# Second-layer experts ranked on chip and run as a straight list of token tiles

## The chip, the cores and the metric

One core of one Trainium2 chip runs the whole program. The core has five engines with queues of their own: TensorE (PE, matmuls and transposes), VectorE (DVE), ScalarE (ACT), GpSimd (POOL) and SyncE (SP, which here only issues transfers). The metric is the device time of one execution in microseconds; the time of a kernel is the median over its runs.

## What is computed

Three stages follow each other: block-causal attention, a first layer that takes the maximum of three products, and a second layer in which each token goes to one of eight experts, or to none.

```python
# attention: B=4, H=8, S=576, D=64, blocks of 64
scores = where(block_i >= block_j, q @ k.T / sqrt(D), -1e9)
x = softmax(scores) @ v                       # -> 2304 tokens x 512
# first layer (d_ff 768)
h = maximum(maximum(x @ w1, x @ w2), x @ w3)
x = h @ w_out
# second layer: N=2304, D=512, E=8, F=1024
do_compute = (x @ w_skip) > 0                 # other tokens pass through
logits = xc @ w_gate
e_idx = argmax(logits, axis=1)
gate_w = softmax(logits)[e_idx]
for e in range(E):                            # tokens of this expert
    y[mask] = gate_w * (maximum(xc[mask] @ w1[e], 0) @ w2[e])
out[do_compute] = xc + y
```

How many tokens an expert gets depends on the inputs. With the inputs of these runs, worked out from the reference, 532 of 2304 tokens are computed, and the experts hold 0, 0, 153, 69, 60, 116, 17 and 117 of them.

## The kernel before

Products keep more of fp32's precision by splitting each operand into a rounded part `hi` and a rest `lo`, and adding three products (hi x hi, hi x lo, lo x hi). A tile is 128 tokens.

The first layer runs in nine chunks of 256 tokens (0 to 8), and its steps are interleaved with the attention of the following chunks by a scheduler that fills all engines. `moe_steps` lists the steps of a chunk: `m_h` (L339, 18 steps of 12 matmuls), `m_logits` (L363), `m_y` (L375, two `y` tiles written to the DRAM tensors `x2` and `out`), `r_gate` (L393, chooses expert and gate) and `r_rank` (L423). `r_rank` gives each token a place in its expert's part of a DRAM table (2304 places for each expert) and scatters token number and gate there; `cum16` holds the counts so far. Chunk 7's two `y` are put off into chunk 8, behind its `m_h`, where they cover chunk 8's ranking (L466 to L475).

The second layer is the class `Moe2`. A weight quarter is 512 x 512 numbers, 1 MB; an expert has four (s = 0, 1 of w1 and 2, 3 of w2). SP loads a quarter into `raw` (L606), ACT makes `hi` (L651), and DVE and POOL each make half of `lo` (L655). While chunk 8's `m_h` runs, `before_step` (L623) loads the first quarters, in the order of expert numbers, and splits the first six: those of expert 0 and half of expert 1. The rings hold six `hi`, six `lo` and six `raw`.

After the last `y`, the counts come out of a matmul (L565), every engine loads all eight into registers (L753), POOL gathers the tokens of the first experts from `x2` (L663), and then a loop that is written out over the eight experts runs under branches: an expert with no token is skipped, one with more than 128 gets a second tile (L783), one with more than 256 a loop. The work on a tile is `products` (L690): the token tile is transposed on PE (L671), ACT and DVE make its two parts out of PSUM (L673, L674), 24 matmuls make the hidden tile in two halves, each half is put through a relu (L703, L710) and transposed and split in the same way, and 24 matmuls make `psy`. The expert's own quarters 2 and 3 are split at the head of its tile and quarters 0 and 1 of the next expert inside it. `finish` (L726) adds and scatters the result to `out` by POOL.

From `_run` on (L737) the order is the one in which the code is written; each engine takes its instructions in that order.

Of the kernel before, what the change touches and what calls it, by code (L numbers as in the profile page):

```python
# [21 lines left out]
P = 128  # L22
# [26 lines left out]
def kernel(  # L49
# [23 lines left out]
    table = dram.tile([NE * CAP, 2], F32, name="table")  # L73

# [10 lines left out]
    counts = const.tile([1, NE], I32, name="counts")  # L85
# [5 lines left out]
def _moe1_phase(tc, nc, const, small, g):  # L91
# [3 lines left out]
    wr_sb, x2, table, out, counts = (g[n] for n in ("wr_sb", "x2", "table", "out", "counts"))  # L95
# [6 lines left out]
    with ExitStack() as st_y:  # L102
# [21 lines left out]
        hid = [[ypool.tile([P, NF, CH], F32R, tag=n, name=n) for n in ("h_h", "h_l")]]  # L124
# [238 lines left out]
        def m_logits(c, rd):  # L363
            h_h, h_l = hid[c // (NCH - 1)]
# [10 lines left out]
        def m_y(c, t, mid=None):  # L375
# [3 lines left out]
            h_h, h_l = hid[c // (NCH - 1)]  # L379
# [64 lines left out]
        def moe_steps(c):  # L444
# [11 lines left out]
            if c < NCH - 2:  # L456
                m_y(c, 0)
                yield
                r_gate(c, rd)
                m_y(c, 1)  # L460
                yield
                r_rank(c, rd)
            elif c == NCH - 2:
                r_gate(c, rd)
                yield
                r_rank(c, rd)  # L466
            else:
                r_gate(c, rd)
                m_y(c - 1, 0, lambda: r_rank(c, rd))
                yield  # L470
                m_y(c - 1, 1)
                yield
                m_y(c, 0)
                yield
                m_y(c, 1)  # L475
# [10 lines left out]
        def constants():  # L486
# [7 lines left out]
            nc.vector.tensor_copy(cum16, base8)  # L494
            nc.vector.tensor_copy(tri, g["cst_sb"][:, P:2 * P])
# [3 lines left out]

        queue = []  # L500
# [351 lines left out]
```

## Time and profile before

| | us |
|---|---|
| median of 3 runs | 754.44 |
| lowest and highest run | 746.52 and 754.82 |
| the profiled execution | 756.49 |
| its span, first to last instruction | 754.7 |
| PE busy in it | 683.6 (91%) |
| DVE, ACT, POOL busy | 474.8, 359.6, 332.6 |

In the profile, times count from the first instruction. "PEclk" is the clock that was granted to TensorE, as a share of full speed. "Idle before" names the time an engine stood still ahead of a row and what released it. An engine counts as busy while it executes an instruction, also when that instruction is held up by another engine.

### The profile page before, as it was taken

How to read it: one execution, taken by the hardware profiler on the slowest of the kernel's cores; microseconds unless marked ns; L12 is line 12 of the kernel's file. 1: busy time of each engine (PE TensorE's matmuls, PEld its weight loads, DVE VectorE, ACT ScalarE, POOL GpSimd, SP SyncE). 2: the span in 40 equal slices, each digit the busy share in tenths (PEclk: the TensorE clock that was granted, in tenths of full speed). 3: DMA queues.
4: the chain of work that ended last, by engine and by line, in shares of the span. 5: the costliest groups of instructions: out<-in, count | busy, mean ns of one | idle time of the engine just before them, and what ended most of it. 6: DMA issues, size and time to landing. Idle time of an engine off the chain costs nothing. (4 is left out here: it accounts for less than half of the span.)

```text
span 754.7 us, 13850 instructions
## 1 busy us (share of the span) xinstructions
PE 683.6 (91%) x4774; PEld 574.4 (76%) x4774; DVE 474.8 (63%) x1307; ACT 359.6 (48%) x941; POOL 332.6 (44%) x422
## 2 busy tenths in 40 slices
PE   7698978999999999999999999999999945988885
PEld 4456756688889889889979979989988834766663
DVE  5899995643456667576657658766547305466574
ACT  4565664243446455555445455644446114364451
POOL 4677775354445222312102133211109528487773
PEclk9989887599999999999999999999999986998899
DMA  7753441242132133322022153111027939757720
GB/s 193 200 159 127 128 132 41 69 123 77 50 99 57 35 102 80 117 99 64 26 64 66 33 147 120 39 64 48 18 95 263 341 113 311 265 173 262 261 80 30
DMA packets 82435, 89.98 MB, mean 119 GB/s; under 512 B 10588, under 2 KB 59132, under 8 KB 82344
## 3 DMA queue, kind: packets, MB, share of 16 engines
q1 hardware_dynamic: 78680, 83.39, 35.5%
q0 software_dynamic: 2624, 5.45, 2.2%
q8 instruction: 47, 0.77, 0.4%
q14 instruction: 44, 0.36, 0.1%
q10 hardware_dynamic: 1040, 0.01, 0.1%
HBM read 78.14 MB, written 11.96 MB: 119 GB/s over the span
## 5 line engine op out<-in xcount | busy, mean ns | idle before, releaser
L348 PE MATMUL ps_h<-x,w 128*128 128x256 f32 x1944 | 282.0, 295 | 1.9 <-DVE hm L355 1.7
L348 PEld LDWEIGHTS ps_h<-x,w 128*128 128x128 f32 x1944 | 254.1, 196 | 11.6 <-issue 5.3
L283 ACT ACTIVATE p<-sc,nm 64x288 f32<-64x288 f32 (+9 forms) x192 | 95.5, 500 | 54.0 <-DVE nm L280 12.4
L276 DVE TENSOR_REDUCE nm<-sc 64x1 f32<-64x288 f32 (+9 forms) x192 | 85.1, 450 | 50.0 <-PE sc L271 30.2
L316 PE MATMUL tp<-cst_sb,p 128*128 128x128 f32 (+1 forms) x480 | 91.4, 282 | 14.8 <-DVE r L299 4.9
L655 POOL TENSOR_TENSOR lo<-raw,hi 128x1024 fp32r<-128x1024 f32 x30 | 81.7, 2741 | 17.5 <-ACT hi L651 8.5
L316 PEld LDWEIGHTS tp<-cst_sb,p 128*128 128x128 f32 (+1 forms) x480 | 57.7, 145 | 36.2 <-issue 15.4
L333 PE MATMUL pv<-pT,vt 128*64 128x128 f32 (+1 forms) x960 | 77.2, 281 | 4.5 <-ACT pT L318 3.9
L360 POOL TENSOR_TENSOR h_l<-hm,h_h 128x256 fp32r<-128x256 f32 x54 | 43.6, 808 | 80.3 <-ACT h_h L359 74.0
L655 DVE TENSOR_TENSOR lo<-raw,hi 128x1024 fp32r<-128x1024 f32 x30 | 66.3, 2222 | 14.1 <-ACT hi L651 13.0
L302 POOL TENSOR_TENSOR p<-p,r 128x128 f32<-128x128 f32 (+8 forms) x72 | 58.9, 820 | 35.4 <-DVE r L299 26.4
L651 ACT CAST hi<-raw 128x2048 fp32r<-128x2048 f32 x30 | 56.4, 1903 | 31.0 <-PEq L783 17.8
L333 PEld LDWEIGHTS pv<-pT,vt 128*64 128x64 f32 x960 | 53.0, 142 | 22.5 <-issue 6.1
L244 POOL TENSOR_TENSOR kl<-kq,kh 64x512 fp32r<-64x512 f32 (+3 forms) x36 | 36.7, 1019 | 64.5 <-ACT kh L243 58.5
L318 ACT COPY pT<-tp 128x256 f32<-128x256 f32 (+4 forms) x112 | 44.7, 401 | 28.8 <-PE tp L316 27.9
L287 POOL MEMSET p<- 128x64 f32 (+1 forms) x96 | 14.3, 153 | 99.8 <-PE tp L316 91.5
L320 DVE COPY pT<-tp 128x256 f32<-128x256 f32 (+4 forms) x80 | 35.4, 447 | 29.0 <-PE tp L316 28.2
L265 PE MATMUL sc<-kn,kq 73*64 73x288 f32 (+4 forms) x96 | 46.5, 594 | 5.5 <-DMA kq<-in_kq_dram 5.2
L269 PE MATMUL sc<-kh,q 128*128 128x288 f32 (+9 forms) x144 | 48.5, 343 | 1.7 <-ACT p L283 1.7
L336 DVE TENSOR_TENSOR x<-pv,x 128x128 fp32r<-128x128 f32 (+1 forms) x80 | 21.6, 270 | 38.4 <-ACT x L335 38.4
L385 PE MATMUL ps_y<-wo_h,h_h 128*128 128x512 f32 x108 | 44.5, 412 | 0.0
L271 PE MATMUL sc<-kl,q 128*128 128x288 f32 (+9 forms) x144 | 43.5, 308 | 0.0
(146 smaller groups left out, 1149.1 us busy)
## 6 DMA issues: line engine op xcount, KB each, us to landing
raw<-in_m_w_dram SPq DMA_DIRECT2D x32, 1024.0 KB
raw<-in_w_dram SPq DMA_DIRECT2D x18, 512.0 KB
kq<-in_kqT_dram SPq DMA_DIRECT2D x16, 512.0 KB
vt<-in_v_dram SPq DMA_DIRECT2D x16, 320.0 KB
x<-y SPq DMA_DIRECT2D x18, 256.0 KB
out_dram<-y SPq DMA_DIRECT2D x18, 256.0 KB
raw<-in_w_out_dram SPq DMA_DIRECT2D x6, 512.0 KB
kq<-in_kqT_dram SPq DMA_DIRECT2D x8, 384.0 KB
```

What stands on the lines that cost most here:

```text
L265: nc.tensor.matmul(ps[:nq, 0:hi - lo], gd["raw"][0:KN, j, q0:q0 + nq], kn_all[hp][0:KN, j, lo:hi], start=True, stop=True)
L269: nc.tensor.matmul(ps[:nq, 0:hi - lo], gd["q1"][:, j, q0:q0 + nq], gd["kh"][:, j, lo:hi], start=True, stop=False)
L276: nc.vector.tensor_reduce(nm[:nq, n:n + 1], pss[n][:nq, 0:hi - lo], axis=AX.X, op=ALU.max, negate=True)
L283: nc.scalar.activation(pt[:nq, lo:hi], pss[n][:nq, 0:hi - lo], AF.Exp, bias=nm[:nq, 0:1], scale=0.125 if b == 0 else 1.0, accum_out=su[:nq ...
L302: nc.gpsimd.tensor_tensor(pt, pt, r[:nq, 0:1].to_broadcast([nq, nk]), op=ALU.mult)
L316: nc.tensor.transpose(tp[:, t, 0:nq], h["p"][:nq, (t0 + t) * P:(t0 + t + 1) * P], ident[:nq, :nq])
L318: nc.scalar.copy(pT[:, t0:t0 + n, 0:nq], tp[:, 0:n, 0:nq])
L333: nc.tensor.matmul(pv[64 * jj:64 * jj + 64, 0:nq], vt[:, t, 64 * jj:64 * jj + 64], hd[k - 1 + jj]["pT"][:, t, 0:nq], start=(t == 0), stop= ...
L348: nc.tensor.matmul(ps, a[:, d, :], x[:, d, :], start=(n == 0), stop=(n == 3 * ND - 1))
L385: nc.tensor.matmul(ps, a[:, f, hs], x[:, f, :], start=(n == 0), stop=(n == 3 * NF - 1))
L651: self.nc.scalar.copy(self.w(e, s)[0], self.raw_of(4 * e + s))
L655: eng.tensor_tensor(lo[:, r], self.raw_of(4 * e + s)[:, r], hi[:, r], op=ALU.subtract)
```

## The change

The second layer no longer runs over experts but over a list of token tiles. It is planned on DVE, from counts that a matmul with a full `ones` puts on all partitions:

- After chunk 6's ranking (1792 tokens) `Plan.rank` orders the experts by their count so far. The numbers of the first three go to SP's registers, and the weights of tiles 0 to 2 are loaded from addresses in these registers, while chunk 8 runs.
- After chunk 7's ranking `Plan.first` notes whether the first expert has at least 128 tokens by then. The rows of its first tile are read from the table and gathered from the first 2048 rows of `x2` during chunk 8 (`Moe2.first`). If it has fewer, that tile's result is sent out of range and its tokens are done again later.
- After chunk 8 `Plan.rest` makes the list of all remaining tiles: expert, place in the table, and the number of tiles.
- Seven tiles (`NS`) run in straight code: the early one, one each for the second and third expert, and four of the list. Any further tile runs in a loop, under the only branch left. Tiles of one expert no longer share its loaded weights.
- Quarters are taken in the order of `seq`, in which quarter 3 of a tile stands behind quarter 0 of the next. `split_hi` is written five and `split_lo` four quarters ahead; DVE now makes 320 of 512 columns of `lo` and POOL 192 (256 each for the first six).
- Chunk 7's `y` go back into chunk 7, and the second copy of the hidden tile (`hid`) goes.

```diff
-            if c < NCH - 2:
+            if c < NCH - 1:
                 m_y(c, 0)
                 yield
                 r_gate(c, rd)
                 m_y(c, 1)
                 yield
                 r_rank(c, rd)
-            elif c == NCH - 2:
...
+                if c >= NCH - 3:
+                    ps = ps_m.tile([P, NE], F32, tag="mo", name="ps_c")
+                    nc.tensor.matmul(ps, ones, cum16, start=True, stop=True)
+                    (plan.rank if c == NCH - 3 else plan.first)(ps)
             else:
                 r_gate(c, rd)
...
+                m_y(c, 0, lambda: r_rank(c, rd))
...
+        m2.first()
         for n in range(3 * NF):
             m2.before_step(n)
             run_moe()
         m2.before_step(3 * NF)
         with tc.manual_schedule():
+            run_moe()
+            run_moe()
+            m2.ready()
+            m2.run(run_moe)
...
+    def first(self, ps):
+        v = self.nc.vector
+        cnt = self.counts(ps, "key")
+        fl, c0 = self.tile("fl", [P, 2]), self.tile("c0", [P, NE])
+        v.tensor_tensor(c0, self.pm[:, 0, :], cnt, op=ALU.mult)
+        v.tensor_reduce(fl[:, 0:1], c0, axis=AX.X, op=ALU.add)
+        v.tensor_scalar(fl[:, 0:1], fl[:, 0:1], float(P), None, op0=ALU.is_ge)
+        v.tensor_scalar(fl[:, 1:2], fl[:, 0:1], -BIG, BIG, op0=ALU.mult, op1=ALU.add)
...
+    def rest(self, ps, pool):
...
+        v.tensor_tensor(big[0], st, inner(off), op=ALU.is_ge)
+        v.tensor_tensor(big[1], st, inner(end), op=ALU.is_ge)
+        v.tensor_tensor(big[0], big[0], big[1], op=ALU.subtract)
...
+        self.seq = [(0, 0), (0, 1), (0, 2)]
+        for k in range(1, self.NS):
+            self.seq += [(k, 0), (k - 1, 3), (k, 1), (k, 2)]
+        self.seq.append((self.NS - 1, 3))
...
+    def reg(self, ap, top):
+        return self.nc.values_load(ap, engines=[mybir.EngineType.SP], min_val=0, max_val=top)
...
+    def load_q(self, e, s, raw):
+        if s < 2:
+            src = self.m2_w1[bass.ds(e, 1), :, s * 512:(s + 1) * 512]
...
+    def first(self):
+
+        nc, plan = self.nc, self.plan
+        self.load_raws(3)
+        self.rows(0, self.reg(plan.pi[0:1, 3:4], (NE - 1) * CAP))
...
+        self.gather(0, NT - CH)
...
+    def split_lo(self, q, m):
+        (hi, lo), raw = self.w(q), self.raw_of(q)
+        for eng, a, b in ((self.nc.vector, 0, m), (self.nc.gpsimd, m, 512)):
+            eng.tensor_tensor(lo[:, :, a:b], raw[:, :, a:b], hi[:, :, a:b], op=ALU.subtract)
...
+    def ready(self):
+
+        ps = self.ps_m.tile([P, NE], F32, tag="mo", name="ps_c")
+        self.nc.tensor.matmul(ps, self.ones, self.cum16, start=True, stop=True)
+        self.g0()
+        self.plan.rest(ps, self.right)
+        for t in (1, 2):
+            self.rows(t, self.reg(self.plan.pi[0:1, 3 + t:4 + t], (NE - 1) * CAP))
+
+    def run(self, last_y):
...
+        self.index(1, 3)
+        self.gather(1)
+        self.gather(2)
...
+        for j, (k, s) in enumerate(self.seq):
+            if s == 0 and k > 0:
+                turn_h(k - 1, 1)
+            if s == 1 and k > 0:
+                turn_h(k, 0)
+            if s == 2 and 0 < k < NS - 1:
+                turn_x(k + 1)
...
+            mm(0, 6)
+            if (k, s) == (0, 1):
+                turn_h(0, 0)
+            if (k, s) == (0, 2):
+                turn_x(1)
...
+            mm(6, 12)
+            if 6 <= j + 5 < len(self.seq):
+                self.split_hi(j + 5)
+            if 6 <= j + 4 < len(self.seq):
+                self.split_lo(j + 4, 320)
...
+            if j < NS - 3:
+                t = 3 + j
+                self.expert[t] = self.reg(li[0:1, 2 * j:2 * j + 1], NE - 1)
+                self.rows(t, self.reg(li[0:1, 2 * j + 1:2 * j + 2], (NE - 1) * CAP + NT - P))
+            self.load_raws(j + 11)
...
+            if 6 <= j < 3 + NS:
+                self.gather(j - 3)
+        self.loop(T, h)
```

The change moves instructions. On PE, just behind the last `y` matmul of chunk 8, the kernel before has (the first operand behind an arrow is the moving one, the second the stationary one; `Two_h`, `Two_l` are the two parts of a transposed tile):

```order
L385 MATMUL ps_y<-wo_l,h_h 128x512
L565 LDWEIGHTS ones
L565 MATMUL ps_c<-cum_69,ones 1x8
L753 TENSOR_LOAD counts x8
L758 COMPARE_AND_BRANCH
L671 MATMUL psa_7844<-cst_sb,xgs_8294 128x128 x4
L758 UNCONDITIONAL_BRANCH x2
L763 COMPARE_AND_BRANCH
L687 MATMUL psa_7844<-hi_7835,Two_h 128x512 x4
```

and the changed kernel has there (`x0h`, `x0l` are the parts of the early tile `xg`, `h` a half of its hidden tile):

```order
L387 MATMUL ps_y<-wo_l,h_h 128x512
L824 LDWEIGHTS ones
L824 MATMUL ps_c<-cum_70,ones 128x8
L783 MATMUL pst_7870<-cst_sb,xg_7864 128x128 x4
L795 MATMUL psa_7868<-hi_7856,x0h 128x512 x4
L795 MATMUL psa_7868<-hi_7856,x0l 128x512 x4
L795 MATMUL psa_7868<-lo_8135,x0h 128x512 x4
L795 MATMUL psa_7869<-hi_7857,x0h 128x512 x4
L795 MATMUL psa_7869<-hi_7857,x0l 128x512 x2
L783 MATMUL pst_7870<-cst_sb,h_8590 128x128 x4
```

The register loads and branches are gone from there, the early tile's transposes follow the last `y` at once, and the first transposes of `h` stand a quarter and a half behind them.

On DVE, the kernel before has between chunk 8's last count and its first relu:

```order
L438 TENSOR_TENSOR cum_69<-cum_69,oh_8312 128x8 x2
L751 TENSOR_SCALAR tg<-tt 128x16
L752 CAST ti<-tt 128x16
L566 SCALAR_TENSOR_TENSOR counts<-cst_sb,ps_c 1x8
L753 TENSOR_LOAD counts x8
L757 MEMSET psy 128x512
L758 COMPARE_AND_BRANCH
L674 TENSOR_TENSOR Two_l<-psa_7844,Two_h 128x512
```

The changed kernel has in the same place the 26 operations of the list, of which the last rows are shown, then the two of `index`, and only then the relu that PE's transposes of `h` wait for:

```order
L654 TENSOR_REDUCE lf<-plan_8535 128x28
L655 TENSOR_TENSOR plan_8536<-plan_8534,d 128x224
L656 TENSOR_REDUCE lf<-plan_8536 128x28
L657 SCALAR_TENSOR_TENSOR lf<-steps,lf 128x28
L658 CAST li<-lf 128x56
L659 CAST li<-end 128x1
L660 TENSOR_SCALAR miss<-steps,end 128x28
L818 CAST ti<-tt 128x2
L819 TENSOR_SCALAR tg<-tt 128x2
L875 TENSOR_SCALAR h_8590<-psa_7868 128x512
L787 TENSOR_TENSOR Two_l<-pst_7870,Two_h 128x512
```

The list thus stands ahead of the index of the next gathers and of the first relu on the same queue.

On POOL, while chunk 8's first layer runs, the kernel before has splits of the first quarters and the `h_l` of chunk 8 alone:

```order
L439 DMA table<-pair,sloti 18432x2 x2
L655 TENSOR_TENSOR lo_8010<-raw_7832,hi_7835 128x1024
L360 TENSOR_TENSOR h_l<-hm_8006,h_h 128x256
L655 TENSOR_TENSOR lo_8045<-raw_7833,hi_7836 128x1024
L360 TENSOR_TENSOR h_l<-hm_8059,h_h 128x256
L655 TENSOR_TENSOR lo_8082<-raw_7834,hi_7837 128x1024
```

and the changed kernel has the gather of the early tile (`xg`) between them:

```order
L441 DMA table<-pair,sloti 18432x2 x2
L774 TENSOR_TENSOR lo_8135<-raw_7853,hi_7856 128x4x256
L774 TENSOR_TENSOR lo_8170<-raw_7854,hi_7857 128x4x256
L362 TENSOR_TENSOR h_l<-hm_8131,h_h 128x256
L774 TENSOR_TENSOR lo_8207<-raw_7855,hi_7858 128x4x256
L362 TENSOR_TENSOR h_l<-hm_8184,h_h 128x256
L777 DMA xg_7864<-x_63,tg 128x512
L362 TENSOR_TENSOR h_l<-hm_8240,h_h 128x256
```

The gather stands behind the third `lo`, and four of chunk 8's six `h_l` are behind it.

## Rows read from the trace of the kernel before

**Rows 1.** Busy us (x instructions) by stretch: PE, PEld, DVE, ACT, POOL, PEclk, DMA share, GB/s.

```profile
150.00:556.00 406.00, 402.87 (x3298) 356.15 (x3298) 250.50 (x901) 200.52 (x642) 116.53 (x230) 1.00 0.24 72
556.00:593.00 37.00, 34.90 (x289) 32.83 (x287) 20.11 (x40) 17.30 (x24) 26.03 (x14) 0.95 0.76 258
613.00:632.00 19.00, 1.44 (x5) 1.10 (x6) 5.03 (x6) 5.22 (x5) 12.42 (x10) 0.57 0.56 173
```

**Rows 2.** Timeline, last y to first tile: start us, us, engine, line, [idle before, releaser].

```profile
612.23 0.39 PE L385 MATMUL ps_y<-wo_l,h_h 128*128 128x512 f32 x1
...
612.70 0.59 ACT L388 COPY y<-ps_y 128x512 f32<-128x512 f32 x1 [3.53 <-PE ps_y L385]
612.75 0.15 DVE L566 SCALAR_TENSOR_TENSOR counts<-cst_sb,ps_c 1x8 int32<-1x8 f32 x1 [4.03 <-PE ps_c L565]
...
617.05 0.48 DVE L757 MEMSET psy<- 128x512 f32 x1 [4.16 <-issue]
617.59 1.00 POOL L663 DMA_INDIRECT xgs<-x,tg  x1 [16.30 <-DVEq L758]
...
621.77 0.75 DVE L728 SCALAR_TENSOR_TENSOR xo<-psy,tt,xgs 128x512 f32<-128x512 f32 x1 [4.23 <-DMA xgs<-x,tg]
...
631.65 2.05 PE L687 MATMUL psa<-hi,Two_h 128*128 128x512 f32 x4 [4.42 <-PEq L783]
```

**Rows 3.** Timeline, the last matmuls.

```profile
747.61 1.09 PE L687 MATMUL psy<-lo,Two_h 128*128 128x512 f32 x4
```

**Rows 4.** Timeline of PE inside expert 2's second tile.

```profile
652.05 1.09 PE L687 MATMUL psb<-hi,Two_h 128*128 128x512 f32 x4
...
652.98 0.63 PE L687 MATMUL psb<-hi,Two_l 128*128 128x512 f32 x2
...
654.34 1.09 PE L687 MATMUL psb<-lo,Two_h 128*128 128x512 f32 x4
```

**Rows 5.** The tile raw, who reads it: ns min/median/max, first and last start.

```profile
L651 ACT CAST hi<-raw x30: 1889/1902/1934, 562.7 to 734.6; 128x2048 fp32r<-128x2048 f32 x30
L655 DVE TENSOR_TENSOR lo<-raw,hi x30: 1215/1254/6023, 569.5 to 736.6; 128x1024 fp32r<-128x1024 f32 x30
L655 POOL TENSOR_TENSOR lo<-raw,hi x30: 2361/2422/3442, 569.7 to 739.2; 128x1024 fp32r<-128x1024 f32 x30
```

**Rows 6.** Timeline, DVE and POOL at the same time.

```profile
665.20 0.69 DVE L703 TENSOR_SCALAR h<-psa 128x512 f32<-128x512 f32 x1 [0.31 <-PE psa L687]
...
697.28 1.23 DVE L655 TENSOR_TENSOR lo<-raw,hi 128x1024 fp32r<-128x1024 f32 x1 [0.32 <-ACT hi L651]
697.47 1.86 POOL L663 DMA_INDIRECT xg<-x,tg  x1 [0.30 <-issue]
...
736.63 6.02 DVE L655 TENSOR_TENSOR lo<-raw,hi 128x1024 fp32r<-128x1024 f32 x1
736.84 4.73 POOL L655 TENSOR_TENSOR lo<-raw,hi 128x1024 fp32r<-128x1024 f32 x2
```

**Rows 7.** Timeline of POOL, first and last of 11 indirect DMAs, first `lo`.

```profile
662.55 0.99 POOL L729 DMA_INDIRECT out_dram<-xo,ti  x1 [8.99 <-DVEq L787]
663.72 6.77 POOL L655 TENSOR_TENSOR lo<-raw,hi 128x1024 fp32r<-128x1024 f32 x2 [0.18 <-ACT hi L651]
...
735.65 1.19 POOL L729 DMA_INDIRECT out_dram<-xo,ti  x1 [0.31 <-issue]
```

**Rows 8.** Timeline of DVE, two dependent small operations.

```profile
597.58 0.17 DVE L418 TENSOR_SCALAR se<-se 128x2 f32<-128x2 f32 x1
597.78 0.17 DVE L419 RECIPROCAL pair<-se 128x2 f32<-128x2 f32 x1
```

**Rows 9.** Timeline, chunk 8's last table scatter and the index made from the table.

```profile
600.32 0.98 POOL L439 DMA_INDIRECT table<-pair,sloti  x1 [0.30 <-issue]
...
608.47 0.17 DVE L751 TENSOR_SCALAR tg<-tt 128x16 int32<-128x16 f32 x1 [9.46 <-DMA tt<-table]
```

**Rows 10.** DMA queues from 556 to 640: GB/s in 40 equal slices.

```profile
GB/s 26 375 101 21 407 395 388 283 49 402 92 407 72 281 277 349 376 386 395 387 385 231 179 1 198 163 145 119 131 8 131 205 203 198 135 365 385 384 388 371
```

More of the change, by code (lines that the diff above doesn't have):

```diff
@@ L94, in _moe1_phase @@
     tri, ones, tid, cum16, wp = (g[n] for n in ("tri", "ones", "tid", "cum16", "wp"))
-    wr_sb, x2, table, out, counts = (g[n] for n in ("wr_sb", "x2", "table", "out", "counts"))
+    wr_sb, x2, table, out, ids, steps = (g[n] for n in ("wr_sb", "x2", "table", "out", "ids", "steps"))
     ws = [g["w1"], g["w2"], g["w3"]]
@@ L582, in __init__ @@
         self.hi = [self.right.tile([P, 4, 512], F32R, name=f"hi{i}") for i in range(6)]
+        self.x0 = [self.right.tile([P, 512], F32R, name=n) for n in ("x0h", "x0l")]
+        self.xg0 = self.right.tile([P, DM], F32, name="xg0")
         self.lo = []
@@ new lines, in finish_t, with g0, index @@
+    def finish_t(self, t):
+        self.finish(self.xg(t), self.ti[:, t:t + 1], self.tt[:, t, 1:2], self.xo[:, t % 3])
+    def g0(self):
+        self.transp(self.xg0, self.pst[0])
+        self.evict(self.pst[0], self.x0)
+    def index(self, a, b):
+        nc = self.nc
+        if a >= 3:
+            nc.vector.tensor_tensor(self.ti[:, a:b], self.tt[:, a:b, 0], self.plan.miss[:, a - 3:b - 3], op=ALU.add)
+        else:
+            nc.vector.tensor_copy(self.ti[:, a:b], self.tt[:, a:b, 0])
+        nc.vector.tensor_scalar(self.tg[:, a:b], self.tt[:, a:b, 0], float(NT - 1), None, op0=ALU.min)
@@ new lines, in loop @@
+    def loop(self, T, h):
+        tc, nc, small, plan, NS = self.tc, self.nc, self.small, self.plan, self.NS
+        n = nc.values_load(plan.li[0:1, 2 * plan.NL:2 * plan.NL + 1], min_val=0, max_val=plan.NL)
+        part = lambda i: [t[:, i] for t in T]
+        with tc.If(n > NS - 3):
+            with tc.For_i(NS - 3, n, 1) as iv:
+                row = small.tile([1, 2], I32, tag="row", name="row")
+                nc.sync.dma_start(out=row, in_=self.tdram[bass.ds(iv, 1), :])
+                e = self.reg(row[0:1, 0:1], NE - 1)
+                for s in range(4):
+                    self.load_q(e, s, self.raw[s])
+                self.rows(0, self.reg(row[0:1, 1:2], (NE - 1) * CAP + NT - P))
+                self.index(0, 1)
+                self.gather(0)
+                for s in range(4):
+                    self.split_hi(s)
+                    self.split_lo(s, 320)
+                self.transp(self.xg(0), self.pst[0])
+                self.evict(self.pst[0], part(0))
+                for s in range(2):
+                    self.mm(self.psa[s], part(0), self.w(s), 0, 12, 0, 12)
+                    nc.vector.tensor_scalar(h[s], self.psa[s], 0.0, None, op0=ALU.max)
+                for s in range(2):
+                    self.transp(h[s], self.pst[s])
+                    self.evict(self.pst[s], part(1 + s))
+                    self.mm(self.psy, part(1 + s), self.w(2 + s), 0, 12, 12 * s, 24)
+                self.finish_t(0)
```

308 lines of the change are left out of this document (144 added, 164 removed).

## The prediction

> **What bounds the kernel now.** I read the busy time by stretch first, then the timeline of the last 200 us, then the rows of single tiles. From 150 to 556 us PE is busy 402.87 of 406 us at a granted clock of 1.00, so that part costs what its matmuls cost; between 613 and 632 us PE works 1.44 us [rows 1]. The last matmul of `ps_y` ends at 612.62, and the first tile of the second layer starts at 631.65. In the 19 us between, the counts go to registers (eight loads, 612.90 to 617.05, 0.52 us each), a gather is issued at 617.59, and its rows are in at 621.77 [rows 2]. The weights loaded and split ahead of 613 belong to experts 0 and 1, of which no tile runs.
>
> Seven tiles then run from 631.65 to 748.70, 16.7 us each [rows 2, 3]. PE does not set that pace: four 128x512 matmuls take 0.93 us (652.05 to 652.98), and a set of four transposes put between adds 0.43 us (652.98 to 654.34 is 1.36, less 0.93) [rows 4]. A tile of 48 matmuls and three such sets is 11.2 + 1.3 = 12.5 us. What sets the pace is the split of the weights. Half a quarter's `lo` takes DVE 1.22 us and POOL 2.40 (the least are 1215 and 2361 ns) [rows 5], and the two shut each other out: DVE's `lo` that started at 736.63 took 6.02, POOL's two from 736.84 took 4.73, and 4.73 + 1.22 = 5.95. DVE's relu out of PSUM ran its 0.69 at 665.20 while POOL was in the `lo` of 663.72. POOL's gather at 697.47, under a `lo` of DVE that began at 697.28, took 1.86 instead of 1.00 [rows 2, 6, 7]. So I count DVE's `lo`, POOL's `lo` and POOL's indirect DMAs as one shared resource. From 662.55 to the end of DVE's `lo` at 742.65 it had 18 quarters to split and 11 indirect DMAs: 18 x 3.62 + 11 x 1.0 = 76.2 of 80.1 us, 95% [rows 5 to 7]. That is the bound of the second layer now.
>
> **The change part by part.**
> *Up to the last y.* On PE the order of attention and first layer stays, but for chunk 7's two `y`, now ahead of chunk 8: their 36 matmuls cost the same wherever they stand. New are the ranking (a dozen small DVE operations), two `ps_c` matmuls, and the wait of the second for `cum16`. Small dependent DVE operations follow each other every 0.20 us [rows 8]; four stand between, so 0.8 us on PE. The first `ps_c` has attention matmuls ahead. The four register loads on SP (2.1 us at 0.52) stand ahead of the last `vt` load, which is asked for a group early. The early gather needs the scatter, table read and index of chunk 7's rank (600.32 to 608.47 for chunk 8's now [rows 9]) and some 4.2 us to land (617.59 to 621.77 [rows 2]), 12.4 in all. Over it lie chunk 8's 216 matmuls of the first layer, at 289 in 37 us [rows 1] about 28 us. I cost it at nothing; without that cover it would hold `h_l` behind it on POOL, and so the logits, up to 12.4 us. Quarter 3's raw load waits on SP behind the same table read, but its split comes later. Last y ends: 612.6 + 0.8 = 613.4.
>
> *From the last y to quarter 3 of the new order* (`seq`; quarters 0 to 2 belong to tile 0). Transposes of `xg0` 0.6, ACT's copy 0.6 [rows 2]: PE starts quarter 0 at 614.6, ends it 2.8 later and half of quarter 1 at 618.8. There it needs `h[0]`, whose relu stands on DVE behind `rest`. DVE has `x0l` at 615.3, then 26 operations of `rest` and 2 of `index`, 28 x 0.20 = 5.6 us, and some 2290 elements beyond the small shapes at 1.19 ns (1.22 us for 1024), 2.7 us: 623.6; the relu 624.3. So PE loses 5.5 us here: this is the new wait. Transposes, second half of quarter 1, first half of quarter 2: 627.7. Gather 1 stands behind the same `rest`, leaves at 623.7 and lands 4.2 later, 627.9. Its transposes, half a quarter and the transposes of `h[1]`: 630.4. After the 19 us pause of now four matmuls take 2.05 instead of 1.09 us [rows 2, 4]; for the shorter pause I add 1.2. Quarter 3 starts at 631.6, where the kernel of before starts quarter 0.
>
> *From quarter 3 to the end.* PE: 25 quarters x 2.79 + 17 sets of transposes x 0.43 = 77.1, to 708.7. Shared resource: 22 quarters are still to be split here (now 24). DVE's part is 320 of 512 columns, 1.22 x 1.25 = 1.52; POOL's 192, 2.40 x 0.75 = 1.80; with 5 scatters and 4 gathers 22 x 3.32 + 9 = 82.0 us. It starts when ACT has `hi` of quarter 6, after its copy of `h[0]`: 625.5 + 1.9 [rows 5] = 627.4. At the 95% of now that is 86.3, so 713.7, and with the last four matmuls 714.8. The two ends lie 6 us apart: the resource decides, not by much. ACT (4 x 1.9 + 4 x 0.6 = 10 a tile) stays under. 17 loads remain from about 625 on; in bursts the queues moved 375 to 407 GB/s [rows 10], 2.7 us for a quarter, and each is asked for some ten quarters ahead of its matmuls: hidden. So are SP's eight register loads for the list, 4.2 us, with which the loads of quarters 11 to 13 queue.
>
> One term hangs on a rule. The row says that a gather under DVE's `lo` takes 1.86 instead of 1.00, so the 9 indirect DMAs stay in the sum [rows 6]. The Trainium skill, page "SBUF — State Buffer", section "Who interferes with whom", states the exclusion for a `tensor_tensor` with two SBUF inputs against GpSimd work that reads SBUF, and holds descriptor generation free of it (marked as inferred). By that the resource would have 73.0 us to do instead of 82.0, and rival A below would be the forecast.
>
> *After the last matmul* now 6.0 us pass (748.70 to 754.7 [rows 3]: `xo`, scatter, landing). The new load of the list's length and its branch lie beside that landing. End 720.8.
>
> **Sum.** 754.7 - 720.8 = 33.9 us off the profiled execution, 756.49 to 722.6. That execution stands 2.05 over the median: 754.44 - 33.9 = 720.5.
>
> **The rivals.**
> (A) *PE is the bound.* If indirect DMAs fit into the gaps of DVE's `lo`, the resource ends at 627.4 + 73.0/0.95 = 704 and PE's 708.7 decides: end 714.7, time 714.4. For it: in the new order a split stands four to five quarters ahead of its matmuls, while now an expert's quarters 2 and 3 are split inside its own tile. Against: the 1.86 us gather.
> (B) *DVE's queue is the bound.* The evictions of transposed tiles stand on DVE between the `lo`s. If each `lo` waits for a whole POOL `lo`, a tile costs DVE 4 x 3.32 + 3 x 0.69 + 0.69 + 0.75 = 16.8 us, 6.25 tiles 105, end 631.6 + 105 + 6.0 = 742.6, time 742.4: within 2%. Against: the median `lo` on DVE is 1254 ns beside a least of 1215 [rows 5], so half of them wait for nothing; with half of them waiting a tile is 13.2 us, the end 720, the forecast again.
> (C) *Slower: loads addressed by register are slow.* Then what remains to be loaded sets the end: 625 + 17 d + 6.5 (split and last matmuls) + 6.0. It meets 754.7 at d = 6.9 us a quarter (152 GB/s), and is over 2% slower from 7.8. Against: loads from fixed addresses on the same queue need 2.7 in a burst [rows 10].
> (D) *The change doesn't do what it says.* Worked out from the reference's routing of its inputs, the experts hold 0, 0, 153, 69, 60, 116, 17, 117 tokens, and expert 2 has 133 of the first 2048. Its early tile counts only from 128 on. Were it missed, the list would hold five tiles instead of four and the loop would run once with nothing hidden: loads 10.8, splits 13, matmuls 12.5, in part side by side, some 30 us: 752, no change.
>
> **How the numbers follow.** Forecast (717 to 728) 0.48, A (708 to 717) 0.22, B and longer waits in the handover (728 to 742) 0.22, C 0.04, D 0.02, anything else slower 0.02. The range takes the forecast, A down to 708 (the runs of before spread over 8 us) and most of B: 708 to 738. 2% is about what a measurement of this kernel can tell from no change: faster than 739.4 has 0.88, within 2% 0.08, slower 0.04.
>
> **What would show it.** Right: PE idle some 5 us near 619 us, released by DVE; `lo` on both engines from about 627 almost without a pause; 12.5 to 14 us a tile; no wait of ACT's `hi` for a load. Wrong: a wait of PE for `Two_l` in every tile (B), `hi` waiting for `raw` (C), instructions of the loop (D), or PE waiting for `h_l` before 605 us, behind the early gather.

## The result, and the profile after

| | before | changed | changed, second set of runs |
|---|---|---|---|
| median, us | 751.86 | 725.19 | 720.92 |
| lowest to highest | 746.52 to 754.82 | 715.62 to 731.36 | 717.40 to 725.72 |
| ratio to before, with its 95% interval | | 0.957 (0.944 to 0.971) | 0.959 (0.952 to 0.966) |
| the profiled execution, and its span | 756.49, 754.7 | 731.36, 729.5 | 725.72, 723.9 |

Some executions are disturbed and several us longer; the medians hold them, the ratios leave them out. Forecast were 720.5 us in a range of 708 to 738, and faster. The profile in the first column of the changed kernel is from the longest of its four executions; it is the one quoted, and the second is named where it differs.

The stages of the changed kernel, as windows with busy time by engine (as [rows 1]: PE, PEld, DVE, ACT, POOL, PEclk, DMA share, GB/s): chunk 8's first matmul to the last y, the handover to quarter 3, quarter 3 to the last matmul.

```profile
576.99:619.25 42.26, 38.96 (x276) 35.62 (x277) 20.63 (x44) 16.43 (x22) 28.27 (x19) 0.96 0.82 297
619.25:635.23 15.98, 11.96 (x53) 9.27 (x52) 8.79 (x33) 5.54 (x7) 3.77 (x3) 0.89 0.36 112
635.23:724.74 89.51, 80.44 (x371) 63.93 (x369) 77.31 (x54) 50.49 (x45) 60.08 (x31) 0.96 0.63 215
```

PE is busy 12 of the 16 us of the handover, where it had 1.44 of 19 [rows 1]. The tail is where PE still loses most: 9.1 us idle of 89.5, at a granted clock of 0.96.

The handover as a timeline (answers [rows 2]):

```profile
618.86 0.39 PE L387 MATMUL ps_y<-wo_l,h_h 128*128 128x512 f32 x1
...
620.42 0.69 DVE L787 TENSOR_TENSOR x0l<-pst,x0h 128x512 fp32r<-128x512 f32 x1 [6.51 <-ACT x0h L786]
620.44 1.20 PE L795 MATMUL psa<-hi,x0h 128*128 128x512 f32 x4 [0.68 <-ACT x0h L786]
621.03 0.15 DVE L588 SCALAR_TENSOR_TENSOR key<-cst_sb,ps_c 128x8 f32<-128x8 f32 x1
...
627.41 0.16 DVE L819 TENSOR_SCALAR tg<-tt 128x2 int32<-128x2 f32 x1
627.48 0.68 DVE L875 TENSOR_SCALAR h<-psa 128x512 f32<-128x512 f32 x1
628.22 0.66 PE L783 MATMUL pst<-cst_sb,h 128*128 128x128 f32 x4 [3.34 <-DVE h L875]
628.36 0.99 POOL L777 DMA_INDIRECT xgs<-x,tg  x1 [12.15 <-DVE h L875]
```

Quarter 0 starts 1.2 us after the last y. The forecast stall is there: the list and the index hold DVE from 621.03 to 627.48, and PE waits 3.34 us for the relu behind them.

The costliest such place of the tail, as a timeline:

```profile
663.75 2.04 POOL L777 DMA_INDIRECT xgs<-x,tg  x1 [0.16 <-issue]
...
665.47 7.07 DVE L774 TENSOR_TENSOR lo<-raw,hi 128x1280 fp32r<-128x1280 f32 x1
665.80 5.37 POOL L774 TENSOR_TENSOR lo<-raw,hi 128x768 fp32r<-128x768 f32 x3
...
672.46 0.68 DVE L875 TENSOR_SCALAR h<-psa 128x512 f32<-128x512 f32 x1
673.19 1.11 PE L783 MATMUL pst<-cst_sb,h 128*128 128x128 f32 x4 [5.12 <-DVE h L875]
```

DVE's `lo` started 0.33 us ahead of POOL's three, but while POOL's gather still ran (663.75 to 665.79). It took 7.07 us and ended behind all three; the relu of the fourth tile stood behind it, and PE waited 5.12. The longest of PE's waits from 560 us on (us in total, times, longest; the 2.3 is a wait for the last `h_l` but one of chunk 8, which the profile puts down to the small write that POOL makes right behind it):

```profile
PE pst L783 <- DVE h L875: 10.7, 4, 5.1
PE ps_l L371 <- POOL xgs L759: 2.3, 1, 2.3
PE psy L795 <- DVE Two_l L787: 1.4, 1, 1.4
PE psa L795 <- ACT x0h L786: 0.7, 1, 0.7
```

And who reads the tile `raw` (answers [rows 5]):

```profile
L769 ACT CAST hi<-raw x28: 1897/1916/1925, 578.3 to 705.6; 128x2048 fp32r<-128x2048 f32 x28
L774 POOL TENSOR_TENSOR lo<-raw,hi x28: 1794/1924/3450, 580.3 to 709.4; 128x768 fp32r<-128x768 f32 x22, 128x1024 fp32r<-128x1024 f32 x6
L774 DVE TENSOR_TENSOR lo<-raw,hi x28: 1226/1942/7068, 580.8 to 713.1; 128x1280 fp32r<-128x1280 f32 x22, 128x1024 fp32r<-128x1024 f32 x6
```

POOL's 768 elements take 1.79 at least (1.80 were estimated). No `hi` of the tail waits for its load, and there are 28 splits: the loop did not run.

### The profile page after: what moved, and what is told of

Read it like the earlier page. It is cut to its first block, busy times and chain, and to the rows that moved or that the text cites. A ratio compares the mean times of both kernels' runs of the same rounds, so it can differ in the third digit from the quotient of the medians.

```text
span 729.5 us, 13695 instructions
## 1 busy us (share of the span) xinstructions
PE 681.2 (93%) x4776; PEld 567.7 (78%) x4776; DVE 488.6 (67%) x1346; ACT 355.3 (49%) x939; POOL 306.5 (42%) x410
## 5 line engine op out<-in xcount | busy, mean ns | idle before, releaser
L350 PE MATMUL ps_h<-x,w 128*128 128x256 f32 x1944 | 277.1, 292 | 2.7 <-ACT x L337 1.9
L350 PEld LDWEIGHTS ps_h<-x,w 128*128 128x128 f32 x1944 | 250.4, 193 | 11.8 <-issue 4.2
L318 PE MATMUL tp<-cst_sb,p 128*128 128x128 f32 (+1 forms) x480 | 93.6, 283 | 9.2 <-DVE x L338 4.1
L335 PE MATMUL pv<-pT,vt 128*64 128x128 f32 (+1 forms) x960 | 79.6, 284 | 4.3 <-ACT pT L320 4.2
L362 POOL TENSOR_TENSOR h_l<-hm,h_h 128x256 fp32r<-128x256 f32 x54 | 45.6, 844 | 78.5 <-ACT h_h L361 72.3
L774 DVE TENSOR_TENSOR lo<-raw,hi 128x1280 fp32r<-128x1280 f32 (+1 forms) x28 | 70.8, 2528 | 4.1 <-ACT hi L769 4.1
L774 POOL TENSOR_TENSOR lo<-raw,hi 128x768 fp32r<-128x768 f32 (+1 forms) x28 | 61.6, 2223 | 8.6 <-ACT hi L769 8.5
L322 DVE COPY pT<-tp 128x256 f32<-128x256 f32 (+4 forms) x80 | 35.4, 447 | 30.6 <-PE tp L318 29.8
L769 ACT CAST hi<-raw 128x2048 fp32r<-128x2048 f32 x28 | 53.0, 1913 | 4.4 <-DMA raw<-in_m_w_dram 3.1
L267 PE MATMUL sc<-kn,kq 73*64 73x288 f32 (+4 forms) x96 | 44.9, 577 | 8.3 <-DMA kq<-in_kq_dram 5.5
L387 PE MATMUL ps_y<-wo_h,h_l 128*128 128x512 f32 x108 | 44.8, 414 | 0.0
```

Of the source, the lines that this page charges most:

```text
L318: nc.tensor.transpose(tp[:, t, 0:nq], h["p"][:nq, (t0 + t) * P:(t0 + t + 1) * P], ident[:nq, :nq])
L335: nc.tensor.matmul(pv[64 * jj:64 * jj + 64, 0:nq], vt[:, t, 64 * jj:64 * jj + 64], hd[k - 1 + jj]["pT"][:, t, 0:nq], start=(t == 0), stop= ...
L350: nc.tensor.matmul(ps, a[:, d, :], x[:, d, :], start=(n == 0), stop=(n == 3 * ND - 1))
L362: nc.gpsimd.tensor_tensor(h_l[:, f, :], prev, h_h[:, f, :], op=ALU.subtract)
L387: nc.tensor.matmul(ps, a[:, f, hs], x[:, f, :], start=(n == 0), stop=(n == 3 * NF - 1))
L769: self.nc.scalar.copy(self.w(q)[0], self.raw_of(q))
```

## The experiments

All are edits of the changed kernel. The time from the start to the last y differs by up to 17 us between executions (last section), so the stretch from the last y to the last matmul, read in each profile, decides: 105.5 us in the first profile of the changed kernel, 103.7 in the second (136.1 before, from 612.62 to 748.70 us). Every other kernel has one profile, so a difference of about 2 us tells nothing. "Lo stretch" is from the start of the tail's first `lo` to the end of its last.

| kernel | median, us | ratio to before (95%) | last y to last matmul | lo stretch |
|---|---|---|---|---|
| changed | 725.19 | 0.957 (0.944 to 0.971) | 105.5 | 83.2 |
| after_again | 720.92 | 0.959 (0.952 to 0.966) | 103.7 | 81.4 |
| relu_first | 717.70 | 0.956 (0.950 to 0.961) | 103.8 | 82.2 |
| all_dve | 709.80 | 0.946 (0.942 to 0.950) | 93.3 | 66.4 |
| half_half | 737.85 | 0.976 (0.966 to 0.986) | 115.5 | 89.9 |
| lead_down | 724.11 | 0.964 (0.955 to 0.972) | 104.1 | 90.0 |
| scatter_late | 720.62 | 0.959 (0.952 to 0.966) | 102.6 | 80.3 |
| rest_late | 725.10 | 0.966 (0.960 to 0.971) | 107.7 | 88.8 |
| list_early | 713.93 | 0.952 (0.944 to 0.960) | 101.2 | 82.2 |
| no_early | 732.54 | 0.974 (0.963 to 0.985) | 114.1 | 81.6 |
| list_early_dve | 710.04 | 0.947 (0.939 to 0.955) | 89.6 | 66.4 |
| all_lo_dve | 706.23 | 0.938 (0.930 to 0.945) | 89.6 | 66.4 |

### The tail: the amount of work, or its order

**relu_first**, DVE's order alone:

```diff
+            if s == 0:
+                nc.vector.tensor_scalar(h[0], self.psa[0], 0.0, None, op0=ALU.max)
             if 6 <= j + 5 < len(self.seq):
                 self.split_hi(j + 5)
...
-            if s == 0:
-                nc.vector.tensor_scalar(h[0], self.psa[0], 0.0, None, op0=ALU.max)
```

> One edit in the straight tiles: the relu of the first hidden half stands on DVE ahead of the `lo` of that step, not behind it. In the changed kernel the last y ends at 619.25 us, quarter 3 starts at 635.23 and the last matmul ends at 724.74, 89.5 us later, where PE's work is 77.1; PE waits for that relu 3.34 us in the handover and 1.30, 5.12 and 0.96 us in the tail. Theory S (the shared resource of DVE's `lo`, POOL's `lo` and POOL's indirect DMAs sets the end): the splits fill 83.2 us with 82 us of work whatever stands between them, so the wait moves from the relu to the `lo`s and quarter 3 to the end changes by less than 2 us. Theory Q (DVE's queue sets it: the relu is late because it stands behind a `lo` that POOL holds up): the three waits of the tail go, 7.4 us and some of the clock behind the longest, and the stretch from quarter 3 to the last matmul falls to 80 to 83 us.

Quarter 3 to the last matmul took 88.9 us (89.5 and 88.8 unchanged): theory Q falls. PE's waits from 600 us on:

```profile
PE psy L795 <- DVE xo L800: 3.6, 1, 3.6
PE pst L783 <- DVE h L871: 3.4, 1, 3.4
PE psy L795 <- DVE Two_l L787: 3.2, 1, 3.2
```

The relu is waited for in the handover only; an `xo` and a `Two_l` are late in its stead, the latter behind a `lo` of DVE that started under a scatter of POOL (658.95 to 661.08) and lasted through the four `lo` behind it (timeline):

```profile
660.71 8.95 DVE L774 TENSOR_TENSOR lo<-raw,hi 128x1280 fp32r<-128x1280 f32 x1
661.08 7.23 POOL L774 TENSOR_TENSOR lo<-raw,hi 128x768 fp32r<-128x768 f32 x4
...
670.32 2.08 PE L795 MATMUL psy<-hi,Two_l 128*128 128x512 f32 x4 [3.21 <-DVE Two_l L787]
```

**all_dve** and **half_half**, the amount:

```diff
-        for eng, a, b in ((self.nc.vector, 0, m), (self.nc.gpsimd, m, 512)):
+        for eng, a, b in ((self.nc.vector, 0, m), (self.nc.gpsimd, m, 512))[:1 + (m < 512)]:
...
-                self.split_lo(j + 4, 320)
+                self.split_lo(j + 4, 512)
```

In half_half only the last number changes, to 256.

> One size changed: in the straight tiles DVE makes all 512 columns of each `lo` (320 before) and POOL none. DVE needs 1.48 us for 320 columns, so 2.37 for 512, where DVE and POOL together need 1.48 + 1.80. Theory S: the shared resource has 22 x 2.37 + 9 = 61 us to do instead of 82 and is no bound any more; PE's 77.1 us decide, and quarter 3 to the last matmul falls from 89.5 to 78 to 82 us. Theory Q by itself: DVE's own queue becomes longer (22 x 0.9 = 20 us more for its engine), each relu stands behind a `lo` of 2.4 us, about what an unhindered one of now with one POOL `lo` takes (3.3), and only the waits above 2.5 us go: 84 to 87 us. A third case, DVE as the bound: its 22 `lo`, 19 second parts, 7 relus and 7 sums are 22 x 2.37 + 19 x 0.69 + 7 x 0.68 + 7 x 0.74 = 75 us, under PE's 77.

> One size changed back: in the straight tiles DVE and POOL make 256 columns of each `lo` each, as in the kernel before. Theory S: 22 x (1.23 + 2.40) + 9 = 88.9 us on the shared resource instead of 82, so 6 to 7 us more from quarter 3 to the last matmul, 95 to 97. If PE were the bound (rival A) or DVE's own time, which falls by 22 x 0.3 us, the stretch would stay at 89.5 or fall by up to 3.

With DVE alone, quarter 3 to the last matmul took 77.3 us, and PE's waits behind the last y are these:

```profile
PE pst L783 <- DVE h L875: 3.4, 1, 3.4
PE psa L795 <- ACT x0h L786: 0.7, 1, 0.7
```

PE is the bound of the tail there. With halves the stretch took 98.2 us, a little more than the 95 to 97 expected, and the lo stretch 89.9 (22 x 3.63 + 9 = 88.9). So less work of POOL on the `lo` is worth 12 us and more costs 9, while DVE's other order in relu_first is worth nothing.

all_dve also prices POOL's indirect DMAs. Its POOL makes no `lo`, and its gather and scatter under a `lo` of DVE read (timeline):

```profile
636.90 0.96 POOL L777 DMA_INDIRECT xgs<-x,tg  x1 [1.93 <-DVE tg L819]
637.14 2.28 DVE L774 TENSOR_TENSOR lo<-raw,hi 128x2048 fp32r<-128x2048 f32 x1
638.17 2.07 POOL L777 DMA_INDIRECT xgs<-x,tg  x1 [0.30 <-issue]
...
658.14 2.28 DVE L774 TENSOR_TENSOR lo<-raw,hi 128x2048 fp32r<-128x2048 f32 x1
658.38 2.92 POOL L801 DMA_INDIRECT out_dram<-xo,ti  x1 [6.28 <-DVE Two_l L787]
```

The gather that starts 0.24 us before the `lo` takes 0.96, and the `lo` beside it the 2.28 of every `lo` here: neither holds the other. The next gather starts under the `lo` and takes 2.07: it ends at 640.24, 0.82 behind the `lo`. The scatter ends 0.88 behind its own. So a DMA that starts under a `lo` of DVE is held until about its end; one that is under way is not, and does not hold the `lo`.

**lead_down** asks why the changed kernel's last matmul comes 10 us behind its last `lo`:

```diff
-            if 6 <= j + 4 < len(self.seq):
-                self.split_lo(j + 4, 320)
+            for q in range(6, len(self.seq)):
+                if j == 2 + (q - 6) * 24 // 21:
+                    self.split_lo(q, 320)
+                    split = q
...
-            self.load_raws(j + 11)
+            self.load_raws(min(j + 11, split + 7))
```

> Only the places of the tail's `lo` change, and with them each load that refills the buffer that a `lo` has read: the 22 `lo` keep their 320 and 192 columns and stand four quarters ahead of their matmuls at first, three from quarter 13, two from quarter 20 and one for the last (four for all in the changed kernel). The changed kernel's last `lo` ends 95.4 us after the last y and its last matmul 105.5 (103.7 in the second profile): 10 us or four quarters of PE later. Theory L (the shared resource paces the tail, and since relu and second parts stand on DVE behind a `lo` that is four quarters ahead, PE is held to that pace and cannot use up the lead): with the lead going down PE runs ahead of the splits, the `lo`s end when they did, 94 to 97 us after the last y, and the last matmul comes 2 to 4 us behind them: 97 to 100 us. Rival (PE's pace is its own, from its waits and clock, whatever the lead): the last matmul stays at 103 to 106 us, and the `lo`s end later, near 101.

Theory L falls: the last matmul came 104.1 us behind the last y, the last `lo` at 102.6. The splits got later, PE not faster; DVE had `lo`s of 6.7, 7.0 and 4.9 us in this order too. (A first form, lead_short, without the second edit, took the `lo` of later quarters from buffers that had been refilled, so it waits for other loads; its time, 726.90, is not used.)

**scatter_late** takes POOL's waits away (`finish` in two parts, the scatter of a tile two quarters later):

```diff
             if s == 3:
-                self.finish_t(k)
+                self.finish(k)
+            if j >= 2 and self.seq[j - 2][1] == 3:
+                self.scatter(self.seq[j - 2][0])
```

> One thing moved: each tile's scatter stands on POOL two quarters later, behind two more `lo`, where its `xo` has long been made; no work is added or taken away. In the changed kernel POOL stands idle 14.1 us at four scatters, waiting for `xo` from DVE, and another 4.8 behind a `Two_l`, while `hi` for its next `lo` are there; afterwards it makes up to four `lo` in a row (5.4 to 11.6 us), and DVE's `lo` beside them take 4.7 to 7.1 us instead of 1.48. Theory H (what holds PE up are these long holds of DVE: the relu or `Two_l` behind them is late, whichever stands there; the earlier orders of DVE only changed which one): without POOL's waits there are fewer runs of three and four, DVE's long `lo` mostly go, and the last matmul comes 94 to 100 us behind the last y instead of 105.5 and 103.7. Theory S (the sum on the shared resource): the same 82 us are to be done, so the last matmul stays within 2 us, 102 to 105.

102.6 us: within what theory S gives, and not what H gives. The hold at the fourth tile's relu is still there, and as long:

```profile
664.72 7.10 DVE L774 TENSOR_TENSOR lo<-raw,hi 128x1280 fp32r<-128x1280 f32 x1
665.09 5.38 POOL L774 TENSOR_TENSOR lo<-raw,hi 128x768 fp32r<-128x768 f32 x3
...
672.48 1.11 PE L783 MATMUL pst<-cst_sb,h 128*128 128x128 f32 x4 [5.51 <-DVE h L879]
```

### The handover

**rest_late** puts index, gathers and list behind the first relu:

```diff
-        self.plan.rest(ps, self.right)
+        self.ps_c = ps
...
+            if j == 0:
+                self.index(1, 3)
+                self.gather(1)
+                self.gather(2)
+                plan.rest(self.ps_c, self.right)
```

> One edit in the handover: the index of gathers 1 and 2, these gathers, and the list of tiles with its write are put behind the relu of the first hidden half, in the order relu, index and gathers, list. In the changed kernel that relu runs at 627.48 behind 26 operations of the list, PE waits 3.34 us for it, and gather 1 leaves at 628.36. Theory: relu at the end of quarter 0's matmuls (some 4.5 us after the last y instead of 8.2), gather 1 some 6 us after the last y instead of 9.1; PE's wait of 3.3 goes, and quarter 3 starts 12 to 13 us after the last y instead of 16.0. By theory S the splits of the tail start as much earlier, and the end comes 3 to 4 us earlier. Rival: the list comes 1 us later, so the loads of the last four tiles do; if a `hi` in the tail then waits for its load, or DVE waits for the table rows inside index and the list behind them, the gain is under 1 us.

The relu ran 4.3 us behind the last y instead of 8.2, but the list then stood ahead of the `Two_l` behind it, and PE waited there (timeline):

```profile
635.88 0.23 DVE L660 TENSOR_SCALAR miss<-steps,end 128x28 f32<-128x28 f32 x1
...
636.02 0.69 DVE L787 TENSOR_TENSOR Two_l<-pst,Two_h 128x512 fp32r<-128x512 f32 x1
636.76 1.22 PE L795 MATMUL psy<-hi,Two_l 128*128 128x512 f32 x2 [6.15 <-DVE Two_l L787]
```

A rival that the expectation had not named: the stall had moved. The last matmul came 107.7 us behind the last y, 2.2 and 4.0 later than in the two profiles unchanged, where 3 to 4 earlier were expected. **list_early** puts the list where DVE stands idle:

```diff
             run_moe()
+            m2.count()
             run_moe()
             m2.ready()
```

`count` holds the `ps_c` matmul and the list's first 18 operations; the last 8 stand behind `g0`, index and gathers behind the first relu.

> One edit in the handover, another place for the list than in rest_late: the second count matmul stands between the two y of chunk 8, most of the list (18 operations) runs under the second y, the last 8 behind the `x0l` of the early tile, and the index and gathers 1 and 2 behind the relu of the first hidden half. In the changed kernel DVE stands idle 6.5 us ahead of `x0l`. Theory (the handover's stall is the list's 8 us on DVE's queue, and rest_late only moved it from the relu to the `Two_l` behind, 6.1 us of PE's wait): with the list under the y, PE's wait of 3.3 us for the relu falls to under 1, no wait for `Two_l` comes in its place, gather 1 leaves some 6.5 us after the last y instead of 9.1. By theory S (the shared resource sets the end) the first split of the tail starts 3 us earlier and so does the end: last y to last matmul 102 to 103.5 us instead of 105.9. Rival: the resource then waits in the tail for what comes no earlier (weights, `hi`), and nothing is gained, as in rest_late (108.1).

101.2 us, 4.3 and 2.5 less than the two profiles unchanged; no wait for the first relu, none for a `Two_l` at that place. The gain lies in the handover, 12.5 us to quarter 3 instead of 16.0 and 14.9; the tail took 88.8.

**no_early** undoes the early tile: its table rows, index and gather move behind chunk 8's ranking.

```diff
-        self.gather(0, NT - CH)
...
+        self.rows(0, self.base0)
...
+        self.gather(0)
         self.g0()
```

> One part of the change undone: the early tile is not gathered during chunk 8; its table rows are read and its tokens gathered behind chunk 8's ranking, as those of tiles 1 and 2 are. Weights, order and split stay. In the changed kernel quarter 0 starts at 620.44, 1.2 us after the last y, and the relu behind the list runs at 627.48. Expected: the list runs first (6.6 us without a pause), the gather leaves some 7 us after the last y and lands 4 to 5 later, so quarter 0 starts 11 to 13 us after the last y. The list is then hidden by that wait, so the relu comes at the end of quarter 0's matmuls, some 7 us later than in the changed kernel, and by theory S the end is 7 to 8 us later, with up to 1.5 more for PE's clock: last y to last matmul 113 to 115 us instead of 105.9. Rival: the tail's splits start as early as before (their weights are there) and take the gain back: under 3 us more.

114.1 us, 8.6 and 10.4 more. PE waits 10.5 us for the rows and no longer for the first relu; quarter 0 starts 12.3 us behind the last y. But the stretch ahead, from chunk 8's first matmul to the last y, took 40.6 us there and 42.3 in the changed kernel: the early gather is not free.

### What the early gather costs, and the two edits that pay

**list_early_dve** joins list_early and all_dve; **all_lo_dve** also gives DVE the first six `lo` whole:

```diff
-            self.split_lo(q, 256)
+            self.split_lo(q, 512)
```

> Both edits that should pay: the list under the second y (as in list_early) and all of the tail's `lo` on DVE (as in all_dve). In all_dve PE works without a pause from quarter 3 to the end; what it loses is 3.4 us for the relu and 0.7 for `x0h`. Theory: PE is the bound there, so every us of the handover comes off the end: last y to last matmul 93.7 - 3.4 = 90 to 91 us, and a median of 705 to 707 us instead of 709.8. Rival: on DVE, which has 75 us of work in the tail, list and `lo` of 2.4 us stand in each other's way and the gain is under 1 us.

> list_early_dve with one size more changed: DVE makes the first six `lo` alone too (all 512 columns, 256 before), so POOL makes none at all. In every kernel with the early gather PE waits 2.3 + 0.3 us for chunk 8's last `h_l`, which stand on POOL behind the early gather and `lo`s of 2.4 us, and 7 to 13 of the y matmuls behind it then come 0.43 us apart instead of 0.23; without the early gather that wait was 0.6 and no y matmul was slow. Theory P (POOL's queue in chunk 8 is the cause): both go, and the stretch from chunk 8's first matmul of the first layer to the last y is 3 to 5 us shorter; behind the last y nothing changes (89 to 90 us to the last matmul), so the median falls by 3 to 5 us. Rival: DVE, which makes `hm` between these `lo`s, now has 6 x 1.1 us more, `hm` comes late behind a `lo` of 2.3 us, and PE waits for it instead: under 1 us of gain.

The joined kernel needed 89.6 us behind the last y, where 90 to 91 were expected. Its median of 710.04 is not the 705 to 707 expected and no better than that of all_dve: in its profile the last y ended at 620.1 us, in that of all_dve at 609.5. POOL's queue in chunk 8 of the changed kernel reads (timeline):

```profile
593.87 1.81 POOL L777 DMA_INDIRECT xg<-x,tg  x1
...
597.43 4.75 POOL L774 TENSOR_TENSOR lo<-raw,hi 128x1024 fp32r<-128x1024 f32 x2
...
603.84 2.35 POOL L774 TENSOR_TENSOR lo<-raw,hi 128x1024 fp32r<-128x1024 f32 x1
...
606.15 0.71 POOL L362 TENSOR_TENSOR h_l<-hm,h_h 128x256 fp32r<-128x256 f32 x1
...
606.92 0.29 PE L371 MATMUL ps_l<-h_l,wp 128*20 128x256 f32 x1 [2.28 <-POOL xgs L759]
```

The gather and the two `lo` make the last `lo` late, and the `h_l` that PE wants stands behind it. With POOL free of `lo`, PE waited 0.6 us for `h_l`, chunk 8 to the last y took 39.2 us instead of 42.3 (43.6 in list_early_dve), and PE works without a pause from quarter 3 on (windows, as above):

```profile
567.67:606.88 39.21, 37.49 (x277) 34.67 (x278) 25.54 (x63) 16.40 (x22) 15.52 (x13) 1.00 0.88 320
606.88:619.14 12.26, 10.35 (x53) 8.08 (x51) 5.47 (x16) 5.53 (x7) 1.94 (x2) 1.00 0.40 114
619.14:696.47 77.33, 77.33 (x371) 62.93 (x369) 67.55 (x54) 50.51 (x45) 15.44 (x10) 1.00 0.69 254
```

706.23 us, ratio 0.938 (0.930 to 0.945): this version is ahead of both kernels.

**after_again** is the changed kernel itself.

> The changed kernel once more, unchanged, beside the kernel before, for a second profile: if the 2.3 us wait for `h_l`, the 3.3 us wait for the first relu and the 5.1 us wait for the fourth relu belong to the kernel, they stand there again, and last y to last matmul is 105 to 106 us again; the time from the start to chunk 0's gate (157.8 us, between 141.6 and 156.2 in the other kernels with the same code up to there) may differ.

The waits stood there again (2.3 for `h_l`, 3.35 for the first relu, 5.1 for the fourth); the last matmul came at 103.7 us where 105 to 106 were expected.

## Why the prediction was right, and where its terms were not

The sum was 720.8 us of span; the two profiles gave 729.5 and 723.9. By its own steps, for the first profile:

- **Last y**: forecast 613.4, measured 619.25. Of these 5.9 us, 4.2 are there at chunk 0's gate (its first `ps_r` matmul), which ran at 157.80 us and in the profile of before at 153.6, in a part that the change leaves alone but for two small constants. The other 1.7 are about what the early gather costs, the term set at nothing: chunk 8 to the last y took 42.3 us, and 40.6 in no_early, with a wait of 2.3 for `h_l` and, behind it, seven y matmuls 0.43 us apart instead of 0.23. (The stretch between scatters too: from the gate to the last y 461 us in one profile, 466 in the other. And no_early is one profile; in the eight profiles that have the gather and PE's order of the changed kernel up to there, lead_short left out, chunk 8 to the last y took 42.2 to 43.8. So they show a cost of some 1.5 us and more; its share of this error is only argued.) The prediction had named that cover and put the wait among the wrong signs, but saw only the 28 us of matmuls, not POOL's `lo`s that stand in the same queue.
- **Handover**: forecast 18.2 us from the last y to quarter 3, measured 15.98. The stall is the one named, the relu behind the list, and 3.34 instead of 5.5: the list took DVE 6.45 us instead of 8.3. A large operation of 224 elements lasts 0.38 us against 0.17 for a small one, 0.21 more and not the 0.27 that 1.19 ns an element gave, and neighbours that don't depend on each other follow in under 0.1.
- **The tail**: forecast 83.2 us from quarter 3 to the last matmul, measured 89.5. Here a step failed. The resource's own part was near: 83.2 us from the first `lo` to the last, forecast 86.3, and the stretch grows with the work (half_half 89.9, 6.7 more where the sum gives 6.9). Part of that nearness is luck. The nine indirect DMAs stand in the sum with 1.0 us each, but all_dve shows that a DMA and a `lo` of DVE share most of that time, and the trace of before showed it too, next to the `lo` of 736.63 that the prediction read (timeline):

```profile
734.35 0.99 POOL L663 DMA_INDIRECT xg<-x,tg  x1
734.73 1.23 DVE L655 TENSOR_TENSOR lo<-raw,hi 128x1024 fp32r<-128x1024 f32 x1 [1.40 <-ACT hi L651]
```

Without the DMAs 22 x (1.48 + 1.79) = 71.9 us of `lo` were done in the 83.2, 86% of it and not the 95% that the sum went by: a term too large and a share too high, which nearly cancel. The step that failed is the end. The sum let the last matmul come 1.1 us behind the last `lo`, though that `lo` stands four quarters ahead of its matmuls; it came 10.1 behind. So 9.0 us too little at the end, 3.1 too much for the stretch, and 0.4 because it began 3.8 us ahead of quarter 3 and not 4.2: the 6.3 by which the tail was longer.
- **The end**: 6.0 us forecast, 4.8 measured.

So 5.9 - 2.2 + 6.3 - 1.2 = 8.8 us over the forecast for this execution (8.7 by the spans), 3.1 for the second; the medians of 725.19 and 720.92 lie 4.7 and 0.4 above 720.5. The direction and the size came out; the terms erred by more than the sum.

**The rivals.** A, PE as the bound, is not how the changed kernel runs (PE waits 10.7 us for relus) but how all_dve does. B named the right place, evictions on DVE behind held `lo`s, and priced it too high: 89.5 us for 25 quarters are 14.3 a tile, not 16.8. C and D did not happen.

**The rule weighed.** The Trainium skill, "SBUF — State Buffer", section "Who interferes with whom", keeps DVE's `tensor_tensor` with two inputs in SBUF apart from GpSimd work that reads SBUF; the traces agree (7.07 us for a 1.48 us `lo`). Its inference that descriptor generation is free of that does not carry over to these indirect DMAs: those that start under a `lo` took 2.04 to 2.92 us in all_dve instead of 0.96 to 1.01 (which of their steps is held, the runs do not tell). So these DMAs belong in the sum, but not with their whole time.

**What stays open.** Four orders of the same work (changed, relu_first, lead_down, scatter_late) end within 102.6 to 105.5 us, though each has other long holds and other waits; in the tail only a change of the amount of work moved the end by more. That the tail follows the amount of `lo` work on the two engines is shown by all_dve and half_half. Why PE's losses add up to the same in each order is not: with lead_down the `lo`s were spread over 90 us, not filled, and the end stayed. Of the 30.6 us by which the stretch behind the last y shrank from the kernel before to the first profile of the changed one, undoing the early gather alone gives 8.6 back, and undoing the new split alone 10.0; what the list, the straight code and the new order of quarters are worth one by one, no run separates.

## What to carry to other kernels

Where two engines shut each other out, count their work as one: moving `lo` to the engine that needs half the time for it was worth 12 us, and reordering the queues nothing that stands clear of the scatter. A small serial computation that moves onto a busy engine's queue is paid for by whatever stands behind it, so look for a stretch in which that engine idles (here under the last y) before you look for an order. When work is issued a fixed lead ahead of its use, the last of it ends that lead before the end: put the lead into the sum.

## What the runs showed of the hardware

- Who is held, DVE or POOL, cannot be told from the two starts that the profile shows. In the first profile of the changed kernel no `lo` of DVE that started with POOL idle was held. In the tail, six started while an indirect DMA of POOL ran that had a `lo` of POOL right behind it. The four that started 0.31 to 0.34 us before the DMA's end were held until the `lo`s behind it were through (3.54 to 7.07 us). The two that started 0.78 us before it took 1.48, and POOL's `lo` was held instead, 2.40 us for the first of the two in the last line here (timeline):

```profile
643.46 1.02 POOL L801 DMA_INDIRECT out_dram<-xo,ti  x1 [2.29 <-DVE xo L800]
643.70 1.48 DVE L774 TENSOR_TENSOR lo<-raw,hi 128x1280 fp32r<-128x1280 f32 x1
644.48 4.21 POOL L774 TENSOR_TENSOR lo<-raw,hi 128x768 fp32r<-128x768 f32 x2
```

- A POOL indirect DMA that starts under DVE's subtraction of two SBUF tiles ends 0.82 to 0.88 us behind it (all_dve); one that started 0.24 us ahead of it took its 0.96.
- Most of the scatter between executions is made near the start: in the eight profiles with PE's order of the changed kernel up to the last y, chunk 0's gate ran at 141.6 to 157.8 us, and from there to the last y it took 460 to 467. The same 173 matmuls up to the gate took 38.74 us in the changed kernel at a mean granted clock of 0.60, and 24.05 in relu_first at 1.00 (0.50 is the 1.2 GHz level), with PE busy nearly all the time (windows; the changed kernel, then relu_first):

```profile
119.06:157.80 38.74, 37.83 (x173) 25.28 (x172) 18.56 (x57) 14.24 (x44) 13.89 (x21) 0.60 0.23 62
```

```profile
117.55:141.60 24.05, 24.05 (x173) 16.74 (x172) 15.21 (x54) 12.94 (x42) 12.04 (x20) 1.00 0.30 84
```

The two lie 1.5 us apart where these windows start and 16.2 at the gate. What lowered the clock in the one is not shown. A change in the last 130 us is better read in the trace from the last y on than in a median.
